# Single slots of an expert kernel: the next slot's rows are split ahead of two other copies, and one slot's row turns come later

## The chip, the core and the metric

The kernel runs on one core of a Trainium2 chip. The core has five engines with a program each: TensorE (PE; its weight loads are PEld), VectorE (DVE), ScalarE (ACT), GpSimd (POOL) and SyncE (SP). They meet only by semaphores, and each takes its own instructions in the order in which they were written. The metric is the device time of one execution in microseconds (us); less is better.

## The reference

Attention with rotary embedding, and behind it a layer of 8 experts of which each token takes one. Cut to what is computed:

```python
batch, n_heads, seq, head_dim = (8, 8, 576, 64)          # 4608 tokens of 512
scores = scale * np.matmul(q_rot, k_rot.transpose(0, 1, 3, 2))
attn = np.exp(scores - np.max(scores, axis=-1, keepdims=True)); attn /= attn.sum(-1, keepdims=True) + 1e-09
x = (attn @ v).transpose(0, 2, 1, 3).reshape(4608, 512)
e_idx = np.argmax(x @ w_gate, axis=1)                     # one expert of 8 for each token
for e in range(8):
    mask = e_idx == e
    h = np.maximum(x[mask] @ w1[e], 0.0)                  # 512 -> 1024
    out[mask] = gate_w[mask, None] * eom[mask, e, None] * (h @ w2[e])   # 1024 -> 512
```

## The kernel before

The first half of the execution is attention; the experts follow, and only they are touched by the change. The tokens of one expert are dealt into **slots**. A double slot takes 256 tokens (two halves h of 128), a **single** slot 128. Slots 0 to 4 are double and gather whole rows of tokens; slots 5 to 22 gather each token in quarters. Of these, 7, 9, 12, 15, 18 and 21 are single, the others double; every single slot is followed by a double one. (Three more slots stand behind a branch that depends on the data.)

All products are made of three float32r products: an operand is split into a high part (a cast on ACT) and a low part (the difference, on DVE), and high times high, low times high and high times low are added up in PSUM. A slot has eight **units** j, each with 512 KB of weights `wr`:

- Units 0 to 3 are the first layer (`first`, `products`): products of the slot's rows `xt` with the weights into `ph`, 24 matmuls a unit in a double slot (L1232, the rows stand as the moving operand in 256 columns), 12 in a single one (L1224). `ph` has two buffers in turn, for even and odd j. In a double slot ACT makes the high part `ht` with the ReLU (L1248) and DVE the low part (L1249); both read `ph`. In a single slot ACT copies the ReLU to `hr` (L1246), and a unit later `across` turns it on TensorE (L1259) and makes the high part on ACT (L1260) and the low part on DVE (L1261).
- Units 4 to 7 are the second layer (`second`, L1274): `ht` with the weights into `py`, 12 matmuls a unit in a double slot, 6 in a single one. After unit 7 `store` scales `py` into `y`, and GpSimd scatters it to the output.

Beside these each unit j of slot s does, in the order of `slot`: `split` of the weights six units ahead (the cast `wh` on ACT, L1159, and the difference `wl` on DVE, L1161), the load of the weights eight units ahead on SP's queue, `turns`, and `gathers`.

`turns` prepares the rows of the slots ahead. A half of gathered rows `xg` is transposed on DVE into `xr` (L1172, by `turned_in`); after the last half `gated` copies the gate factors `gs` (L1184). Then `turn` splits the half: `xt` high on ACT (L1193), `xt` low on DVE (L1194). Splitting is always done for the next slot, half h in unit 4+h, since there is only one `xt`, and the products of the current slot read it until the end of unit 3. The transposes are done two slots ahead in units 6 and 7 if the gather of that slot has been issued whole, and else one slot ahead in units 2 and 3. `gathers` issues up to two quarter gathers (L1118, on GpSimd, 128 tokens each) a unit, eight for a double slot; those of slot i wait until `gs` of slot i-2 is made, since both use one buffer.

Nothing orders the work but this text: the instructions of an engine stand in the order in which `slot` writes them.

Of the kernel before, what the change touches and what calls it, by code (L numbers as in the profile page):

```python
# [77 lines left out]
def list_rows(nb):  # L78
    return -(-nb * S // SLOT) * SLOT


def slot_counts(nb):


    n0 = min(5, -(-((nb - 2) * S - E * (SLOT - 1)) // SLOT)) if nb > 2 else 0
    n0 = max(0, n0)
    T = nb * S - n0 * SLOT
    n2 = max(0, -(-(T - E * P) // SLOT))
    most = (T + E * (P - 1)) // P
    if n2:  # L90
        n2 += 3
    return n0, n2, max(min(E, most - 2 * p) + 2 * max(0, p - n2) for p in range(most // 2 + 1))
# [40 lines left out]
class Small:  # L133


    def __init__(self, p):
        self.p, self.tag = p, "sc"
# [140 lines left out]
class Attention:  # L278
# [117 lines left out]
    def turns(self, g):  # L396
        n, i = divmod(g, 9)
        n -= i == 0
        if 0 <= n < len(self.pairs):
            for units in TURNS.get(i, ()):  # L400
                self.pairs[n].turn(units)


class Pair:
# [49 lines left out]
    def load(self, t):  # L454

        if t:
            self.raw = self.pp2.tile([P, 4, S], F32, tag="raw", name=f"raw{self.nm}")
        self.nc.sync.dma_start(out=self.raw[:, 2 * t:2 * t + 2, :], in_=self.qkd[:, 2 * t:2 * t + 2, :])
# [361 lines left out]
class Moe:  # L820
# [3 lines left out]
    def __init__(self, tc, nb, pools, cc, ident, cnt, w, xd, lists, lst, out):  # L824
        self.tc, self.nc, self.nb, self.NT = tc, tc.nc, nb, nb * S
        self.p1, self.px2, self.small = pools
        self.cc, self.ident, self.cnt, self.w, self.xd, self.lists, self.lst, self.out = cc, ident, cnt, w, xd, lists, lst, out
        self.n0, self.n2, self.n1 = slot_counts(nb)
        self.rows = list_rows(nb) // P
        self.idx, self.ei, self.quarters, self.xr = {}, {}, {}, {}  # L830
        self.due, self.sent, self.asked, self.gss_made = [], [], 0, set()
        self.wr, self.wp, self.xt, self.ht, self.gss, self.pys, self.hrs, self.regs = ({} for _ in range(8))

        self.T = max(1, self.n1 - 3)
        self.todo = [(2, 0, i) for i in range(self.n0)]

        k = 0
        for i in range(self.n2):
            self.todo.append((2, 2, i))
            while k < self.T and k * (self.n2 - 1) < i * self.T:  # L840
                self.todo.append((1, 1, k))
                k += 1
        self.todo += [(1, 1, i) for i in range(k, self.n1)]
        self.nm, self.end = "", self.n0 + self.n2 + self.T
# [255 lines left out]
    def gather(self, s, after=None):  # L1100
        if s >= self.end:
            return
        if not self.whole(s):
            for b in range(4 * self.todo[s][0]):
                self.part(s, b)
            return
        self.mark(self.xgs[s % 2][0:1, 0, 0:1], after)
        n = self.NT - 2 * S
        for h in range(self.todo[s][0]):
            self.nc.gpsimd.indirect_dma_start(  # L1110
                out=self.rows2[s % 2][:, h, :], out_offset=None, in_=self.xd[0:n, :],
                in_offset=bass.IndirectOffsetOnAxis(ap=self.ids(s, h), axis=0), bounds_check=n - 1, oob_is_err=False)
# [10 lines left out]
    def gathers(self, s, j):  # L1123

        if j == 6 and s + 2 < self.end and self.whole(s + 2):
            self.gather(s + 2)
        if j == 0:
            for i in range(max(self.asked + 1, s + 2), min(s + 4, self.end)):
                if not self.whole(i):
                    self.due += [(i, b) for b in range(4 * self.todo[i][0])]  # L1130
                    self.asked = i
        for _ in range(2):
            if self.due:
                i, b = self.due[0]
                if self.todo[i][1] in self.quarters and i - 2 in self.gss_made:
                    self.part(i, b)
                    self.due.pop(0)

    def load(self, u, after=None):
        if u >= 8 * self.end:  # L1140
# [52 lines left out]
        nc.scalar.copy(xth[:, :, hs], xr)  # L1193
        V.tensor_tensor(out=xtl[:, :, hs], in0=xr, in1=xth.bitcast(F32)[:, :, hs], op=ALU.subtract)  # L1194

    def turns(self, s, j):

        for i in (s + 1, s + 2):
            if i >= self.end:
                break  # L1200
            k, near = self.todo[i][0], i == s + 1
            for h in range(k):
                if self.whole(i):
                    now = near and j == h + 4
                else:
                    now = j == h + (2 if near else 6) and i not in self.gss_made
                    now = now and not any(g == i for g, _ in self.due) and (h == 0 or (i, 0) in self.xr)
                if now:
                    self.turned_in(i, h)
                    if h == (0 if self.whole(i) else k - 1):  # L1210
                        self.gated(i)
                if near and j == h + 4:
                    self.turn(i, h)
# [120 lines left out]
    def slot(self, s, left, per=2, last=False):  # L1334
        for j in range(8):
            u = 8 * s + j
            single = self.todo[s][0] == 1
            if j < 4:
                if s or j > 1 or not self.n0:
                    self.first(s, j)  # L1340
            elif not last:
                self.second(s, j - 4)
            if single and 1 <= j <= 4:
                self.across(s, j - 1)
            self.split(u + self.LEAD)
            self.load(u + self.LOADS)
            self.turns(s, j)
            if j == 7:
                self.close(s) if last else self.store(s)
            self.gathers(s, j)  # L1350
            if j == 0 and last:
                self.nc.gpsimd.drain()
            for _ in range(per if s or j > 1 else 1):
                if left:
                    left.pop(0)()
# [67 lines left out]
```

## Time and profile before

| | |
|---|---|
| median of 3 runs | 963.38 us (957.52 to 967.2) |
| the profiled execution | 959.85 us |
| its span, first to last instruction | 958.0 us |
| TensorE matmuls busy | 901.4 us (94%) |
| VectorE busy | 790.5 us (83%) |
| ScalarE busy | 657.4 us (69%) |
| GpSimd busy | 634.9 us (66%) |
| mean granted TensorE clock | 0.995 |

Busy times are averages over both halves of the program; which engine another one waits for at one place is seen in the timeline and in the list of waits. Times in rows count from the start of the span. In timelines a bracket shows how long the engine was idle before the instruction, and what ended that. A row may hold several instructions (x2), and a start-to-start distance is what one instruction costs the engine, since neighbours overlap a little at their ends.

### The profile page before, as it was taken

The page shows a single profiled execution, that of the slowest core. Times are in us where ns is not written, and L with a number is a line of the kernel's source. Part 1 is how long each engine was busy: PE and PEld are TensorE (multiplying, and loading weights), DVE is VectorE, ACT ScalarE, POOL GpSimd, SP SyncE. Part 2 cuts the span into 40 slices and gives each one's busy share as a digit, 9 for nine tenths or more (in the row PEclk, how much of TensorE's full clock was granted, in tenths as well). Part 3 has the DMA queues.
Part 4 walks back from the last instruction along what each step waited for, and adds up shares of the span by engine and source line. Part 5 has one row for each costly group of instructions (what it writes and reads, how often), then busy time and mean ns, then how long its engine had stood idle before and what let it go on. Part 6 is the DMA issues. An engine that isn't in the chain of part 4 may idle for free.

```text
span 958.0 us, 34278 instructions
## 1 busy us (share of the span) xinstructions
PE 901.4 (94%) x14325; PEld 779.5 (81%) x14325; DVE 790.5 (83%) x1456; ACT 657.4 (69%) x1373; POOL 634.9 (66%) x573
## 2 busy tenths in 40 slices
PE   4999998999999999989899999899999999999997
PEld 3777777778877777778788999799889998998986
DVE  6899998999999998989588777668886868778681
ACT  4777788899898988787764544447654657457561
POOL 4898898898989898798211228667847646476120
PEclk9999999999999999999999999999999999999999
DMA  6544565465646646455399957669796878878550
GB/s 239 196 177 143 189 225 200 166 237 188 229 148 228 234 153 212 141 203 176 114 344 309 304 188 233 222 213 308 264 295 230 288 234 274 284 237 275 199 184 21
DMA packets 61183, 208.44 MB, mean 218 GB/s; under 512 B 9512, under 2 KB 11614, under 8 KB 61024
## 3 DMA queue, kind: packets, MB, share of 16 engines
q1 hardware_dynamic: 49920, 183.78, 55.9%
q0 software_dynamic: 9824, 21.27, 6.4%
q8 instruction: 114, 1.87, 0.8%
q10 hardware_dynamic: 1280, 1.15, 0.4%
q14 instruction: 45, 0.37, 0.1%
HBM read 186.09 MB, written 22.43 MB: 218 GB/s over the span
## 4 chain that ended last, share of the span: by engine, by line
PE 63%; DVE 16%; issue 8%; ACT 7%; POOL 3%; DMA 2%; POOLq 0%; DVEq 0%; ACTq 0%
PE ph L1232 17%; PE py L1274 16%; PE acc L569 13%; PE sc L523 10%; DVE pm L532 7%; PE ph L1224 3%; ACT pm L539 3%; DVE pt L547 3%; PE acc L584 2%; DVE pt L545 2%; DVE xb L596 1%; DVE wl L1161 1%; POOL xg L1118 1%; DMA xg<-xd,2qi 1%; ACT ac L576 1%
## 5 line engine op out<-in xcount | busy, mean ns | idle before, releaser
L539 ACT ACTIVATE pm<-pm,m 128x576 f32<-128x576 f32 x288 | 221.7, 770 | 54.8 <-DVE pm L532 51.2
L1161 DVE TENSOR_TENSOR wl<-wr,wh 128x1024 fp32r<-128x1024 f32 x172 | 221.8, 1299 | 31.7 <-ACT wh L1159 29.8
L532 DVE TENSOR_SCALAR_CACHE_REDUCE pm<-sc 128x576 f32<-128x576 f32 x288 | 205.4, 746 | 24.6 <-PE sc L523 19.1
L569 PE MATMUL acc<-pt,v 32*64 32x128 f32 (+1 forms) x9216 | 197.3, 295 | 19.5 <-DVE xb L596 7.7
L1232 PE MATMUL ph<-xt,wh 128*128 128x256 f32 x1088 | 200.7, 286 | 8.1 <-DVE xt L1194 4.3
L1274 PE MATMUL py<-wh,ht 128*128 128x512 f32 x640 | 207.7, 396 | 0.0
L569 PEld LDWEIGHTS acc<-pt,v 32*64 32x64 f32 x9216 | 156.9, 131 | 45.1 <-issue 27.5
L1159 ACT CAST wh<-wr 128x1024 fp32r<-128x1024 f32 x184 | 187.6, 1047 | 0.0
L1232 PEld LDWEIGHTS ph<-xt,wh 128*128 128x128 f32 x1088 | 171.7, 192 | 11.6 <-DVE xt L1194 6.2
L523 PE MATMUL sc<-kq 64*128 64x288 f32 x1536 | 161.1, 320 | 16.4 <-ACT kq L484 9.8
L474 POOL TENSOR_TENSOR raw<-raw,rt 128x1152 f32<-128x1152 f32 x62 | 164.5, 2653 | 0.0
L523 PEld LDWEIGHTS sc<-kq 64*128 64x128 f32 x1536 | 122.0, 190 | 50.5 <-issue 22.2
L1232 PE MATMUL ph<-xt,wl 128*128 128x256 f32 x544 | 155.4, 286 | 0.0
L1118 POOL DMA_INDIRECT xg<-xd,2qi x96 | 120.8, 1259 | 49.7 <-issue 24.1
L1274 PEld LDWEIGHTS py<-wh,ht 128*128 128x128 f32 x640 | 120.4, 188 | 26.1
L1274 PE MATMUL py<-wl,ht 128*128 128x512 f32 x320 | 125.8, 393 | 0.0
L1248 ACT ACTIVATE ht<-ph 128x512 fp32r<-128x512 f32 x68 | 40.6, 597 | 117.8 <-PE ph L1232 117.8
L545 DVE STREAM_TRANSPOSE pt<-pm 128x576 f32<-128x576 f32 x160 | 116.9, 760 | 2.1 <-ACT pm L539 2.1
L1232 PEld LDWEIGHTS ph<-xt,wl 128*128 128x128 f32 x544 | 104.5, 192 | 0.1
L1249 DVE SCALAR_TENSOR_TENSOR ht<-ph,ht 128x512 fp32r<-128x512 f32 x68 | 47.0, 691 | 63.7 <-ACT ht L1248 63.5
L487 POOL TENSOR_TENSOR kq<-raw,kq 128x1152 fp32r<-128x1152 f32 (+1 forms) x33 | 82.5, 2500 | 9.1 <-ACT kq L484 9.0
L547 DVE STREAM_TRANSPOSE pt<-pm 128x1152 f32<-128x1152 f32 x64 | 88.0, 1374 | 0.7 <-ACT pm L539 0.7
(255 smaller groups left out, 1121.3 us busy)
## 6 DMA issues: line engine op xcount, KB each, us to landing
wr<-in_w SPq DMA_DIRECT2D x184, 512.0 KB, 4.6
raw<-in_qk SPq DMA_DIRECT2D x64, 576.0 KB, 4.9
v<-in_v SPq DMA_DIRECT2D x64, 576.0 KB, 6.3
xd<-xb SPq DMA_DIRECT2D x16, 640.0 KB, 4.0
xg<-xd,2qi POOLq DMA_INDIRECT x96, 4.6
xd<-xb SPq DMA_DIRECT2D x8, 160.0 KB, 4.8
rt<-in_rope ACTq DMA_DIRECT2D x1, 576.0 KB, 5.8
xg<-xd,1qi POOLq DMA_INDIRECT x24, 5.0
```

What stands on the lines that cost most here:

```text
L474: self.eng(eng).tensor_tensor(out=rv, in0=rv, in1=rt, op=ALU.mult)
L523: self.nc.tensor.matmul(self.ps[i][:, a, :HS], st, self.kq[r, mov, x], start=(n == 0), stop=(n == 2))
L532: self.nc.vector.tensor_scalar(self.halves(i), self.ps[i][:, :, :HS], 1.0, FAR, op0=ALU.mult, op1=ALU.min, accum_out=self.m[i])
L539: self.nc.scalar.activation(self.pc[i], self.pc[i], AF.Exp, bias=self.m[i], scale=-1.0, accum_out=self.z[:, zi:zi + 1])
L545: self.nc.vector.transpose(out=self.pt[:, c + 5 * h, :], in_=self.pc[units[0]])
L547: self.nc.vector.transpose(out=self.pt[:, c:c + 6:5, :], in_=self.pc[units])
L569: nc.tensor.matmul(self.acc[h * D:h * D + D, a, o:o + 32 * n], self.v[r, h, j, :], self.pt[r, u:u + n, 32 * j:32 * j + 32], start=(j == 0) ...
L1118: self.nc.gpsimd.indirect_dma_start(out=self.xgs[s % 2][:, b, :], out_offset=None, in_=self.xd.rearrange("n (q x) -> (n q) x", x=BW)[0:n, ...
L1159: self.nc.scalar.copy(wh, r)
L1161: eng.tensor_tensor(out=wl, in0=r, in1=wh.bitcast(F32), op=ALU.subtract)
L1232: nc.tensor.matmul(ph[:, f, :], st[:, dc, fs], mv[:, dc, :], start=(n == 0), stop=(n == 11))
L1274: self.nc.tensor.matmul(py[h], st[:, f, hs], mv, start=(f == 0 and n == 0), stop=(f == 7 and n == 2))
```

## The change

Two edits in the slots, with no instruction added or removed.

In single slots `turns` is called twice. For the next slot it is now called ahead of `across` and `split`, so that in units 4 and 5 the split of the next slot's rows stands ahead of the copies of the turned ReLU and of the weight casts of that unit. For the slot after the next the call stays where it was. Double slots keep their order.

`gathers` now notes in `asked_at` the unit in which a slot's last quarter was issued, and the transposes two slots ahead are only made if that was at least three units ago; the old test was that nothing of the slot was still due.

```diff
@@ gather
         if not self.whole(s):
             for b in range(4 * self.todo[s][0]):
                 self.part(s, b)
+            self.asked_at[s] = 8 * s - 8
             return
@@ gathers
                     self.part(i, b)
                     self.due.pop(0)
+                    if not any(g == i for g, _ in self.due):
+                        self.asked_at[i] = 8 * s + j
@@ turns
-    def turns(self, s, j):
+    def turns(self, s, j, ahead):
-        for i in (s + 1, s + 2):
-            if i >= self.end:
-                break
+        for i in (s + a for a in ahead if s + a < self.end):
             k, near = self.todo[i][0], i == s + 1
...
                     now = j == h + (2 if near else 6) and i not in self.gss_made
-                    now = now and not any(g == i for g, _ in self.due) and (h == 0 or (i, 0) in self.xr)
+                    now = now and i in self.asked_at and (near or 8 * s + j - self.asked_at[i] > 2) and (h == 0 or (i, 0) in self.xr)
@@ slot
+            if single:
+                self.turns(s, j, range(1, 2))
             if single and 1 <= j <= 4:
                 self.across(s, j - 1)
             self.split(u + self.LEAD)
             self.load(u + self.LOADS)
-            self.turns(s, j)
+            self.turns(s, j, range(2, 3) if single else range(1, 3))
```

Between the two programs the order differs on VectorE and ScalarE alone. The first place is the end of each single slot; here slot 9 on VectorE, units 3 to 5, before (`ht_9` is the low part of the slot's ReLU, `htp_3` the turned ReLU of unit 3, `xt_10` the rows of the next slot, `xr_0` and `xr_1` their halves):

```order
889 L1161 TENSOR_TENSOR wl_12410<-wr_12355,wh_12409 128x1024
890 L1261 TENSOR_TENSOR ht_9_12294<-htp_3_12422,ht_9_12293 128x2x128
891 L1161 TENSOR_TENSOR wl_12428<-wr_12387,wh_12427 128x1024
892 L1194 TENSOR_TENSOR xt_10_12434<-xr_0_12257,xt_10_12433 128x4x128
893 L1161 TENSOR_TENSOR wl_12444<-wr_12413,wh_12443 128x1024
894 L1194 TENSOR_TENSOR xt_10_12434<-xr_1_12277,xt_10_12433 128x4x128
```

The same place on VectorE with the change:

```order
889 L1164 TENSOR_TENSOR wl_12410<-wr_12355,wh_12409 128x1024
890 L1197 TENSOR_TENSOR xt_10_12423<-xr_0_12257,xt_10_12422 128x4x128
891 L1262 TENSOR_TENSOR ht_9_12294<-htp_3_12426,ht_9_12293 128x2x128
892 L1164 TENSOR_TENSOR wl_12432<-wr_12387,wh_12431 128x1024
893 L1197 TENSOR_TENSOR xt_10_12423<-xr_1_12277,xt_10_12422 128x4x128
894 L1164 TENSOR_TENSOR wl_12446<-wr_12413,wh_12445 128x1024
```

The first half of `xt_10` has passed one `ht_9` and one `wl`, the second half one `wl` more; the second half now has one weight difference less ahead of it. ScalarE at the same place, before:

```order
848 L1159 CAST wh_12409<-wr_12355 128x1024
849 L1260 CAST ht_9_12293<-htp_3_12422 128x2x128
850 L1159 CAST wh_12427<-wr_12387 128x1024
851 L1193 CAST xt_10_12433<-xr_0_12257 128x4x128
852 L1159 CAST wh_12443<-wr_12413 128x1024
853 L1193 CAST xt_10_12433<-xr_1_12277 128x4x128
```

ScalarE with the change:

```order
848 L1162 CAST wh_12409<-wr_12355 128x1024
849 L1196 CAST xt_10_12422<-xr_0_12257 128x4x128
850 L1261 CAST ht_9_12293<-htp_3_12426 128x2x128
851 L1162 CAST wh_12431<-wr_12387 128x1024
852 L1196 CAST xt_10_12422<-xr_1_12277 128x4x128
853 L1162 CAST wh_12445<-wr_12413 128x1024
```

The casts moved in the same way, ahead of the copy of the turned ReLU and of one weight cast each. The second place is slot 6, whose transposes are the only ones that move by the new test: before, they stand on VectorE in units 6 and 7 of slot 4. From unit 7 of slot 4 on, VectorE before (`y_11289` is the output of slot 4's second half):

```order
816 L1161 TENSOR_TENSOR wl_11277<-wr_11223,wh_11276 128x1024
817 L1172 STREAM_TRANSPOSE xr_1_11282<-xg 128x4x4x32
818 L1184 COPY gs_11284<-xg 32x2 x4
819 L1293 TENSOR_SCALAR y_11289<-py_1_11173,gs_10845 128x512
820 L1249 SCALAR_TENSOR_TENSOR ht_5_11305<-ph_0_11306,ht_5_11304 128x512
821 L1161 TENSOR_TENSOR wl_11334<-wr_11243,wh_11333 128x1024
```

VectorE with the change, from unit 7 of slot 4 to unit 3 of slot 5:

```order
815 L1164 TENSOR_TENSOR wl_11275<-wr_11223,wh_11274 128x1024
816 L1294 TENSOR_SCALAR y_11280<-py_1_11173,gs_10845 128x512
817 L1250 SCALAR_TENSOR_TENSOR ht_5_11296<-ph_0_11297,ht_5_11295 128x512
818 L1164 TENSOR_TENSOR wl_11325<-wr_11243,wh_11324 128x1024
819 L1250 SCALAR_TENSOR_TENSOR ht_5_11296<-ph_1_11345,ht_5_11295 128x512
820 L1164 TENSOR_TENSOR wl_11373<-wr_11278,wh_11372 128x1024
821 L1250 SCALAR_TENSOR_TENSOR ht_5_11296<-ph_2_11378,ht_5_11295 128x512
822 L1164 TENSOR_TENSOR wl_11406<-wr_11337,wh_11405 128x1024
823 L1175 STREAM_TRANSPOSE xr_0_11411<-xg 128x4x4x32
824 L1250 SCALAR_TENSOR_TENSOR ht_5_11296<-ph_3_11413,ht_5_11295 128x512
825 L1164 TENSOR_TENSOR wl_11441<-wr_11376,wh_11440 128x1024
826 L1175 STREAM_TRANSPOSE xr_1_11446<-xg 128x4x4x32
```

The two transposes of slot 6 and the copies of `gs` behind them have moved back by four units, behind three or four of the low parts `ht_5` that stood behind them.

## Rows read from the trace of the kernel before

**Rows 1.** Waits of TensorE from 480 us to the end: us, times, longest.

```profile
PE ph L1232 <- DVE xt L1194: 4.3, 6, 0.7
```

**Rows 2.** TensorE's timeline, slot 9 into 10: start, us, engine, line, operation.

```profile
695.07 0.40 PE L1274 MATMUL py<-wh,ht 128*128 128x512 f32 x1
695.30 0.28 PE L1232 MATMUL ph<-xt,wh 128*128 128x256 f32 x1
696.30 0.38 PE L1232 MATMUL ph<-xt,wh 128*128 128x256 f32 x1 [0.71 <-DVE xt L1194]
```

**Rows 3.** TensorE's timeline: first-layer ends of slots 8 and 22, behind singles 7 and 21.

```profile
659.53 0.28 PE L1232 MATMUL ph<-xt,wh 128*128 128x256 f32 x1
...
671.96 0.39 PE L1274 MATMUL py<-wh,ht 128*128 128x512 f32 x1
...
928.37 0.28 PE L1232 MATMUL ph<-xt,wh 128*128 128x256 f32 x1
...
940.74 0.40 PE L1274 MATMUL py<-wh,ht 128*128 128x512 f32 x1
```

**Rows 4.** TensorE's timeline: the first layer of slot 11, behind a double slot.

```profile
718.95 0.40 PE L1232 MATMUL ph<-xt,wh 128*128 128x256 f32 x2
...
730.39 0.40 PE L1274 MATMUL py<-wh,ht 128*128 128x512 f32 x1
```

**Rows 5.** VectorE's timeline at the end of slot 9.

```profile
691.16 1.23 DVE L1161 TENSOR_TENSOR wl<-wr,wh 128x1024 fp32r<-128x1024 f32 x1
692.30 0.42 DVE L1261 TENSOR_TENSOR ht<-htp,ht 128x256 fp32r<-128x256 f32 x1
692.67 1.23 DVE L1161 TENSOR_TENSOR wl<-wr,wh 128x1024 fp32r<-128x1024 f32 x1
693.82 0.68 DVE L1194 TENSOR_TENSOR xt<-xr,xt 128x512 fp32r<-128x512 f32 x1
694.42 1.22 DVE L1161 TENSOR_TENSOR wl<-wr,wh 128x1024 fp32r<-128x1024 f32 x1
695.55 0.69 DVE L1194 TENSOR_TENSOR xt<-xr,xt 128x512 fp32r<-128x512 f32 x1
...
700.37 0.69 DVE L1249 SCALAR_TENSOR_TENSOR ht<-ph,ht 128x512 fp32r<-128x512 f32 x1
```

**Rows 6.** ScalarE's timeline at the end of slot 9.

```profile
690.07 1.06 ACT L1159 CAST wh<-wr 128x1024 fp32r<-128x1024 f32 x1
...
692.54 0.62 ACT L1193 CAST xt<-xr 128x512 fp32r<-128x512 f32 x1
```

**Rows 7.** TensorE's timeline: the first layer of slot 5.

```profile
596.76 0.40 PE L1232 MATMUL ph<-xt,wh 128*128 128x256 f32 x2
...
606.44 0.39 PE L1232 MATMUL ph<-xt,wh 128*128 128x256 f32 x1 [3.76 <-DVE ht L1249]
...
613.80 0.40 PE L1274 MATMUL py<-wh,ht 128*128 128x512 f32 x1
```

**Rows 8.** VectorE's timeline at the end of slot 4.

```profile
603.74 0.71 DVE L1172 STREAM_TRANSPOSE xr<-xg 128x512 f32<-128x512 f32 x1 [3.98 <-DMA xg<-xd,2qi]
...
605.71 0.68 DVE L1249 SCALAR_TENSOR_TENSOR ht<-ph,ht 128x512 fp32r<-128x512 f32 x1
```

**Rows 9.** GpSimd's timeline: three of the gathers of slot 6.

```profile
590.91 1.00 POOL L1118 DMA_INDIRECT xg<-xd,2qi  x1 [0.31 <-issue]
...
593.52 3.55 POOL L1118 DMA_INDIRECT xg<-xd,2qi  x1 [0.30 <-issue]
...
598.68 1.95 POOL L1118 DMA_INDIRECT xg<-xd,2qi  x1 [0.30 <-issue]
```

**Rows 10.** Windows: stretch, length, busy of each engine, granted clock, DMA share, GB/s.

```profile
480.00:500.00 20.00, 20.00 (x125) 17.80 (x125) 15.75 (x28) 13.38 (x19) 2.91 (x3) 1.00 0.98 376
606.40:608.60 2.20, 2.16 (x11) 2.16 (x12) 2.20 (x3) 0.00 (x0) 1.73 (x2) 0.59 0.41 132
624.90:636.50 11.60, 11.60 (x98) 11.60 (x97) 6.50 (x7) 4.73 (x7) 7.62 (x7) 1.00 0.64 202
```

More of the change, by code (lines that the diff above doesn't have):

```diff
@@ L830, in __init__ @@
         self.idx, self.ei, self.quarters, self.xr = {}, {}, {}, {}
-        self.due, self.sent, self.asked, self.gss_made = [], [], 0, set()
+        self.due, self.sent, self.asked, self.gss_made, self.asked_at = [], [], 0, set(), {}
         self.wr, self.wp, self.xt, self.ht, self.gss, self.pys, self.hrs, self.regs = ({} for _ in range(8))
```

## The prediction

> **What bounds the kernel now.** I read the waits of TensorE first, since it has the most work, then its timeline around each wait, then VectorE, ScalarE and GpSimd at the same times. In the experts TensorE hardly pauses, and where it does the reader sees two places. The first comes six times: the first layer of the double slot behind each single slot waits for the low part of its rows, 4.3 us in all and 0.7 each [rows 1]. At slot 10 the first matmul starts at 695.30, needs only the high part, and runs; the second needs the low part and starts at 696.30 [rows 2], where 0.12 us later would have done (three matmuls of a first layer take 0.36 us: 96 of them take 11.44 us in slot 11, behind a double slot [rows 4]). The second place comes once: in slot 5 TensorE waits 3.76 us for VectorE's `ht` [rows 7], and VectorE had itself waited 3.98 us for a gather of slot 6, with this `ht` queued behind the transpose [rows 8].
>
> What each costs is read from the length of a first layer, which also holds what the waits do to the clock. Undisturbed it is 730.39 - 718.95 = 11.44 us [rows 4]. Behind the first single slot it is 671.96 - 659.53 = 12.43, behind the sixth and last 940.74 - 928.37 = 12.37 [rows 3]: 0.96 us more on average, times six 5.8 us. In slot 5 it is 613.80 - 596.76 = 17.04 [rows 7], so 5.6 us more, of which 3.76 are the wait and some 1.8 slower matmuls behind it, at a granted clock of 0.59, near the lower level of 1.2 GHz, where 1.00 is 2.4 GHz [rows 10]. Nothing else on the way to the end is touched, and TensorE's lead is passed on to the end one for one: behind the last slot's first layer stand only its second layer, one copy and the scatter.
>
> **Splits ahead in single slots.** Nothing is added, and on VectorE the queue at the end of slot 9 has no gap, so the new times come from moving its starts about [rows 5]. Start to start, `wl` takes 1.14 us (691.16 to 692.30), `ht` 0.37, `xt` 0.60. Before, the second `xt` starts at 695.55 and ends at 696.24; TensorE goes on 0.06 later. With the change: `wl` 691.16, first `xt` 692.30, `ht` 692.90, `wl` 693.27, second `xt` 694.41, end 695.10. That is 1.14 us earlier, one `wl`. TensorE wants it at 695.30 + 0.12 = 695.42 and can have it at 695.16. So the wait goes whole, with 0.26 us to spare. ScalarE must follow: its cast for the first half can start when `wh` ends at 690.07 + 1.06 = 691.13, takes 0.62 [rows 6] and is done at 691.75, ahead of 692.30. The cast overwrites `xt`, which the products of unit 3 read; that unit was over before TensorE began the 24 matmuls of 0.23 us (695.07 to 695.30 [rows 2]) that end at 695.30, so at about 689.6, and nothing new is waited for.
>
> What is pushed back is the `ht` of unit 3, 0.60 us on VectorE, to end at 693.3. TensorE wants it for the last six matmuls of the slot, which begin at 695.30 - 6 x 0.23 = 693.92: covered by 0.6 us. The weight differences that are passed belong to units six ahead and cost nothing.
>
> What is late next is the `ht` of the following slot's unit 0, at 700.37, ending at 701.06 [rows 5]. VectorE has the same work up to there and no gap in it, so it stays at 701.06 although TensorE comes 0.96 us sooner. It frees one of two `ph` buffers; TensorE wants that for unit 2, two units of 2.86 us behind 695.30, so at 701.02, and gets it at 701.06 + 0.06 = 701.12. Something like 0.1 to 0.2 us is lost again, in the four slots with two halves of rows two slots ahead (9, 12, 15, 18); behind slot 7 only one half is ahead and behind 21 none. I take 4 x 0.15 = 0.6 us. **Gain of this part: 5.8 - 0.6 = 5.2 us;** its bounds are nothing, if the wait only changes its place, and 5.8.
>
> **Slot 6 turned later.** The two transposes and the `gs` copies, some 2 us (from 603.74 to 605.71 stand one transpose, the copies and slot 4's `y` [rows 8]), leave the end of slot 4 for units 2 and 3 of slot 5. VectorE no longer stands in front of a gather that is still under way. What waited for it, `y`, its scatter and `ht`, goes on at once. At the new place the gathers have landed: the last one was there at 603.74 [rows 8], and TensorE ends unit 2 of slot 5 at 596.76 + 3 x 2.86 = 605.3, after which VectorE has an `ht` and a `wl` to make before the first of the transposes. The 2 us there lie beside TensorE's work: in the undisturbed first layer of slot 6 VectorE is busy 6.50 of 11.60 us [rows 10]. GpSimd's gathers of slot 8 use the buffer that these transposes read and can start only behind them, when slot 5 goes into its second layer; behind them in its queue stand slot 5's scatters and the gathers of slot 9. None is wanted before the end of slot 6, a double slot of some 23 us (11.44 for its first layer [rows 4], about as much for its second) later. So the 5.6 us go whole, and with the wait goes the clock's fall.
>
> How much of this is in every execution is the open size. The last gathers of slot 6 came late because one took 3.55 us on GpSimd, where another shortly before took 1.00 [rows 9]. Had it taken 1.00 as well, the wait would have been 2.55 us shorter, with no fall of the clock: 5.6 - 2.55 - 1.8 = 1.2 us. These are the bounds, 1.2 and 5.6. I take 5.6: the long gather starts at 593.52 and ends at 597.07 while VectorE works without a pause on its splits, and the next long one, 598.68 to 600.63 [rows 9], again lies beside a `wl`. That points to a cause in the order of the program and not in chance.
>
> The Trainium skill has the rule for that, in "SBUF — State Buffer", section "SBUF: two separate sides": VectorE and GpSimd share a pair of ports, held for a whole instruction, also by a VectorE operation with two SBUF inputs against a GpSimd one that reads SBUF. By that rule the long gather comes back in each execution and the gain is 5.6 us; without it, 1.2. The trace agrees only in part, since the 1.00 us gather lies beside splits as well.
>
> **The sum.** 5.2 + 5.6 = 10.8 us off the profiled execution, 959.85 - 10.8 = 949.1. That execution lies 3.5 us under the median of the runs, so from the median I expect 963.38 - 10.8 = 952.6 us.
>
> **The rivals.**
> *The gather is seldom so late.* Then only 1.2 us of the second part are there to be won: 5.2 + 1.2 = 6.4, 957.0 us. For it: one row of 3.55 among others of 1 to 2. Against it: the order that surrounds it is the same in every execution.
> *VectorE becomes the bound behind single slots.* The margins of 0.26 us and -0.1 are thin. If transposes and splits run 0.4 us later than moved starts say, half of the six waits comes back, at `xt` or at the following `ht`: 2.9 less, 955.5 us. For it: the queue without a gap from 691.16 to 700.37. Against it: the same instructions, whose total cannot grow by their order.
> *The splits gain nothing* because another wait ends just as late: 963.38 - 5.6 = 957.8 us. Against it: no other wait of TensorE is to be seen at these six places.
> *Slower.* The lower clock comes in at a place where TensorE now works without a pause. At it a first-layer matmul takes up to twice its 0.12 us, so each us of work costs another; from 10.8 us of work at the lower level on, the kernel is slower than before, and with twice that it takes 974 us. Against it: TensorE was busy 20 of 20 us from 480 to 500 at a clock of 1.00 [rows 10], and the waits that go are no rest that it needed there.
>
> **How the numbers follow.** The forecast has 0.56, the seldom late gather 0.17, VectorE as the bound 0.16, no gain from the splits 0.08, slower 0.03. The runs of before spread over 9.7 us, so a median of a few may be off by 2 to 3 us. The range goes from 949.5 (both parts at their upper bounds, 11.4, less a spread of 2.5) to 959 (the rival at 957.0 and 2 us of spread). One per cent, 9.6 us, is about what a measurement of this kernel can tell from no change. The forecast's gain lies only 1.2 us beyond it, so about one in five of its own chance falls short by the spread, and the rivals with smaller gains reach it now and then: faster by over 1% 0.54, within 1% 0.43, slower 0.03.
>
> **What would show it.** In the new profile the six waits of the first layer for `xt` are gone, the first layers behind single slots last about 11.5 us, slot 5's too, the clock is 1.00 around 605 us, and the end of VectorE's second `xt` lies 0.1 to 0.3 us ahead of the first matmul that needs it. A new wait of some 0.1 us for `ht` in unit 2 may stand in four slots. The prediction is wrong if waits for `xt` or `ht` of 0.5 us remain, if VectorE still waits for a gather in slot 5, or if TensorE's clock falls elsewhere.

## The result, and the profile after

The changed kernel takes 951.61 us, the median of 6 runs (946.07 to 953.68), against 960.86 us for 6 runs of the kernel before (957.52 to 967.2). The ratio is 0.9892, with a 95% interval of 0.9859 to 0.9926, so about 1% faster; the two medians differ by 9.25 us, 0.96%. Times here and below are medians of all runs of a kernel, while a ratio and its interval are those of its fast runs and not the quotient of two medians. The forecast was 952.6 us. The profiled execution of the changed kernel took 952.37 us, its span 950.6 us.

The list of waits of TensorE from 480 us to the end holds no first layer any more; one wait of 0.3 us is left, at 522.60, and the kernel before has it as well. The six waits for `xt` [rows 1] and the wait for `ht` of slot 5 [rows 7] are gone:

```profile
PE pl L718 <- DVE xt L1197: 0.3, 1, 0.3
```

TensorE's timeline of the changed kernel shows the first layer of slot 5 (answers to [rows 7]), of slot 10 with its third unit (to [rows 2]) and of slot 22 (to [rows 3]); the last row of each is the start of its second layer:

```profile
599.90 0.40 PE L1233 MATMUL ph<-xt,wh 128*128 128x256 f32 x2
...
611.42 0.40 PE L1275 MATMUL py<-wh,ht 128*128 128x512 f32 x1
...
692.07 0.40 PE L1233 MATMUL ph<-xt,wh 128*128 128x256 f32 x2
...
697.67 0.28 PE L1233 MATMUL ph<-xt,wl 128*128 128x256 f32 x1
697.84 0.51 PE L1233 MATMUL ph<-xt,wh 128*128 128x256 f32 x2
...
703.69 0.39 PE L1275 MATMUL py<-wh,ht 128*128 128x512 f32 x1
...
921.85 0.40 PE L1233 MATMUL ph<-xt,wh 128*128 128x256 f32 x2
...
933.36 0.39 PE L1275 MATMUL py<-wh,ht 128*128 128x512 f32 x1
```

Slot 5 takes 611.42 - 599.90 = 11.52 us where it took 17.04, slot 10 takes 11.62, slot 22 11.51. At 692.07 the first two matmuls run as one group; in [rows 2] the second came 1.00 us behind the first.

VectorE's timeline of the changed kernel at the end of slot 4 (answers to [rows 8]) and of slot 9 (to [rows 5]):

```profile
602.67 0.75 DVE L1294 TENSOR_SCALAR y<-py,gs 128x512 f32<-128x512 f32 x1
603.67 0.69 DVE L1250 SCALAR_TENSOR_TENSOR ht<-ph,ht 128x512 fp32r<-128x512 f32 x1 [0.25 <-ACT ht L1249]
...
611.45 0.70 DVE L1175 STREAM_TRANSPOSE xr<-xg 128x512 f32<-128x512 f32 x1
...
687.93 1.23 DVE L1164 TENSOR_TENSOR wl<-wr,wh 128x1024 fp32r<-128x1024 f32 x1
689.07 0.68 DVE L1197 TENSOR_TENSOR xt<-xr,xt 128x512 fp32r<-128x512 f32 x1
689.67 0.42 DVE L1262 TENSOR_TENSOR ht<-htp,ht 128x256 fp32r<-128x256 f32 x1
690.01 1.22 DVE L1164 TENSOR_TENSOR wl<-wr,wh 128x1024 fp32r<-128x1024 f32 x1
691.14 0.68 DVE L1197 TENSOR_TENSOR xt<-xr,xt 128x512 fp32r<-128x512 f32 x1
...
697.09 0.69 DVE L1250 SCALAR_TENSOR_TENSOR ht<-ph,ht 128x512 fp32r<-128x512 f32 x1
```

In slot 5 the first transpose of slot 6's rows stands at 611.45, behind TensorE's whole first layer, and `y` and the `ht` of the first three units no longer queue behind it. In slot 9 the second `xt` ends at 691.14 + 0.68 = 691.82, ahead of the first product.

ScalarE's casts of `xt` there (answers to [rows 6]) are early enough: the second ends at 690.15, and VectorE needs it at 691.14.

```profile
689.51 0.64 ACT L1196 CAST xt<-xr 128x512 fp32r<-128x512 f32 x1
```

GpSimd's gathers of slot 6 (answers to [rows 9]) still hold a long one, right behind a short one:

```profile
596.46 0.99 POOL L1119 DMA_INDIRECT xg<-xd,2qi  x1 [0.30 <-issue]
597.76 2.79 POOL L1119 DMA_INDIRECT xg<-xd,2qi  x1 [0.30 <-issue]
```

The long one ends at 600.55, 0.95 us behind the start of VectorE's first operation with one input behind the splits, here a small cast with other small operations behind it:

```profile
599.60 0.15 DVE L906 CAST 1idx<-1tr 128x9 int32<-128x9 f32 x1
```

The windows of the changed kernel (answers to [rows 10]; columns as there) have the granted clock at 1.00, the 2.4 GHz level, in the first layer of slot 5 and over the whole of the experts:

```profile
599.90:611.40 11.50, 11.50 (x97) 11.50 (x96) 8.95 (x17) 4.84 (x7) 8.79 (x8) 1.00 0.90 277
...
476.20:933.40 457.20, 456.80 (x2946) 414.66 (x2945) 356.63 (x552) 264.30 (x368) 236.24 (x181) 1.00 0.78 256
```

The two profiled executions differ by 7.5 us, the experts alone by more. From the first product of the experts to the end of the last first layer it was 473.30 to 940.74 before, 467.44 us, and is 476.24 to 933.36 now, 457.12 us: 10.3 us less. The half ahead of the experts, which the change does not touch, took 2.9 us longer in this execution; in the other profiles below its end lies anywhere from 472.07 to 477.91, whatever the order. So the experts' stretch is the better measure of the change in a single profile, and the table of the experiments gives it for each kernel.

### The profile page after: what moved, and what is told of

Same layout as the page of the kernel before. It is cut to its first block, busy times and chain, and to the rows that moved or that the text cites. A ratio compares the mean times of both kernels' runs of the same rounds, so it can differ in the third digit from the quotient of the medians.

```text
span 950.6 us, 34288 instructions
## 1 busy us (share of the span) xinstructions
PE 903.2 (95%) x14325; PEld 782.2 (82%) x14325; DVE 791.8 (83%) x1456; ACT 657.2 (69%) x1373; POOL 635.0 (67%) x573
## 3 DMA queue, kind: packets, MB, share of 16 engines
q8 instruction: 114, 1.87, 0.8%
## 4 chain that ended last, share of the span: by engine, by line
PE 67%; DVE 13%; issue 9%; ACT 5%; POOL 2%; DMA 2%; POOLq 0%; DVEq 0%; ACTq 0%
PE py L1275 18%; PE ph L1233 17%; PE acc L569 14%; PE sc L523 11%; DVE pm L532 6%; PE ph L1225 3%; PE acc L584 2%; ACT pm L539 2%; DVE pt L547 2%; DVE pt L545 2%; DVE xb L596 1%; DMA xg<-xd,2qi 1%; ACT ac L576 1%; PE acc L718 1%; DMA rt<-in_rope 1%
## 5 line engine op out<-in xcount | busy, mean ns | idle before, releaser
L1164 DVE TENSOR_TENSOR wl<-wr,wh 128x1024 fp32r<-128x1024 f32 x172 | 219.5, 1288 | 29.8 <-ACT wh L1162 27.5
L1233 PE MATMUL ph<-xt,wh 128*128 128x256 f32 x1088 | 198.2, 285 | 0.0
L523 PE MATMUL sc<-kq 64*128 64x288 f32 x1536 | 163.1, 323 | 15.9 <-ACT kq L484 9.5
```

Source lines behind the costliest of these rows:

```text
L523: self.nc.tensor.matmul(self.ps[i][:, a, :HS], st, self.kq[r, mov, x], start=(n == 0), stop=(n == 2))
L1164: eng.tensor_tensor(out=wl, in0=r, in1=wh.bitcast(F32), op=ALU.subtract)
L1233: nc.tensor.matmul(ph[:, f, :], st[:, dc, fs], mv[:, dc, :], start=(n == 0), stop=(n == 11))
```

## The experiments

First-layer lengths are start to start, as above; "behind singles" are the six of slots 8, 10, 13, 16, 19 and 22. Ratios are to the kernel before on the same chip. A time marked (one) is that of a single run.

| kernel | time, us | ratio, 95% | slot 5 | behind singles | experts |
|---|---|---|---|---|---|
| before, first profile | 960.86 | 1 | 17.04 | 12.37 to 12.49 | 467.44 |
| before, again | 959.00 (one) | | 15.28 | 12.35 to 12.47 | 465.83 |
| changed, first profile | 951.61 | 0.9892 [0.9859, 0.9926] | 11.52 | 11.51 to 11.63 | 457.12 |
| changed, again | 951.44 | 0.9921 [0.9884, 0.9957] | 11.52 | 11.51 to 11.63 | 456.77 |
| later turning alone | 955.23 | 0.9946 [0.9923, 0.9968] | 11.52 | 12.36 to 12.46 | 461.86 |
| order alone | 955.20 | 0.9950 [0.9930, 0.9971] | 14.00 | 11.52 to 11.62 | 459.64 |
| low part made twice | 954.79 | 0.9952 [0.9917, 0.9988] | 11.51 | 11.94 to 12.35 | 460.70 |
| parts behind the relu copy | 951.95 | 0.9902 [0.9869, 0.9935] | 11.52 | 11.52 to 11.64 | 456.97 |
| fills in slot 4 | 963.52 (one) | | 15.45 | 12.36 to 12.47 | 466.44 |
| transposes in slot 4 | 957.01 (one) | | 13.21 | 12.35 to 12.46 | 464.25 |

**The two halves, a first time.** Four kernels ran together first, on a chip on which the kernel before took 973.21 us (965.8 to 986.43). The first one has the new rule for turning alone:

```diff
-            if single:
-                self.turns(s, j, range(1, 2))
...
-            self.turns(s, j, range(2, 3) if single else range(1, 3))
+            self.turns(s, j, range(1, 3))
```

> Only the new test on the gather; the order in single slots is the old one. My theory: the first layer of slot 5 lasts 11.5 us instead of 17.0, the clock stays at 1.00 there, and the six first layers behind single slots still last 12.4 us with their waits of 0.7 us for xt. About 5.5 us off the time of before (ratio near 0.994). Rival, that the late gather is seldom so late and the profile of before was an unlucky one: the median falls by 1 to 2 us only.

The second has the new order alone, with the old condition:

```diff
-                    now = now and i in self.asked_at and (near or 8 * s + j - self.asked_at[i] > 2) and (h == 0 or (i, 0) in self.xr)
+                    now = now and not any(g == i for g, _ in self.due) and (h == 0 or (i, 0) in self.xr)
```

> Only the order in single slots; the old test on the gather. My theory: the six waits are gone and the six first layers last 11.5 to 11.6 us, in all 5.1 us off (ratio near 0.995); slot 5 keeps its wait, VectorE waits 2 to 4 us for a gather of slot 6, and the first layer of slot 5 lasts 14 to 17 us, with a slower clock behind the wait if that is over 3 us. The rival, chance, expects that the wait in slot 5 is under 1.5 us in this execution, with no gather of slot 6 over 2.1 us on GpSimd.

Measured: 976.66 us, ratio 1.0021 [0.9971, 1.0072], and 970.87 us, ratio 0.998 [0.9939, 1.0021]. The places themselves did mostly as expected: with the rule alone slot 5 took 11.52 and five of the six behind singles 12.35 to 12.47 (one 13.15); with the order alone four of the six took 11.51 to 11.63, the others 12.11 and 12.51. One expectation failed: with the order alone slot 5 took 11.52 us and not 14 to 17, and no gather of slot 6 took over 1.87 us, which is what the rival expected. Slot 4 ahead of it had taken 16.53 us, though, so that in this execution the gathers were done by 595.94, and VectorE's splits began only at 600.82: it does not tell the two apart. Both kernels show waits of TensorE in double slots for which the profile names no releaser, which neither earlier profile has, 7.7 us of them in the first layers of the first kernel and 4.2 us in those of the second. The timed ratios of this pair say nothing on the change as long as these stand in them.

**Only unit 5 early.** The changed kernel, with the early turning in unit 5 of a single slot alone, so that the first half's parts stand where they stood before:

```diff
-            if single:
+            early = single and j == 5
+            if early:
                 self.turns(s, j, range(1, 2))
...
-            self.turns(s, j, range(2, 3) if single else range(1, 3))
+            self.turns(s, j, range(2, 3) if early else range(1, 3))
```

> The changed kernel, but in single slots the split of the next slot's rows is called early in unit 5 only, not in unit 4. My theory: the low part of the second half ends when all that stands ahead of it is done, so only the one weight difference that it passes in unit 5 counts; the first half's place in unit 4 changes nothing. First layers behind single slots last 11.5 to 11.6 us as in the changed kernel, same time as that. The rival, that both moves share the gain, expects 11.9 to 12.0 us at the six places and some 2.5 us more in all.

Measured: 962.31 us, ratio 0.9916 [0.9865, 0.9966]; behind singles 11.51 to 11.68 in four slots, 11.96 and 12.45 in two beside waits without a releaser. Where nothing else disturbs, the one `wl` that the second half passes is enough.

**Nothing turned two slots ahead in a single slot.** The changed kernel with another condition:

```diff
-                    now = now and i in self.asked_at and (near or 8 * s + j - self.asked_at[i] > 2) and (h == 0 or (i, 0) in self.xr)
+                    now = now and i in self.asked_at and (near or self.todo[s][0] == 2 and 8 * s + j - self.asked_at[i] > 2) and (h == 0 or (i, 0) in self.xr)
```

> The changed kernel, but single slots make no transposes two slots ahead; they come in units 2 and 3 of the following double slot. My theory: the 0.1 us by which the first layers of slots 10, 13, 16 and 19 still exceed 11.5 us comes from the low part of ht in unit 0 queued behind two transposes and the copies of gs; with these away, these four last 11.45 to 11.52 us, 0.4 us less in all, too little for the times. The rival, that the rest has another cause (the split itself), expects 11.6 us as before. If the later gathers that hang on gs come too late, a wait for a gather appears in the double slots and the kernel is slower by that.

Measured: 982.49 us, ratio 1.0119 [1.0053, 1.0185]. In two of the four slots, 13 and 19, the first layer took 11.52 and 11.48, as expected; in the two others 12.05 and 11.99. But this kernel has the most of the waits without a releaser, 15.0 us in first layers, in seven places. Row of TensorE's timeline, then of ScalarE's, in slot 6 of this kernel:

```profile
644.82 0.80 PE L1233 MATMUL ph<-xt,wh 128*128 128x256 f32 x2 [3.29 <-issue]
```

```profile
643.44 0.60 ACT L1249 ACTIVATE ht<-ph 128x512 fp32r<-128x512 f32 x1 [5.75 <-remote]
```

TensorE waits for the `ph` that ScalarE's `ht` frees. ScalarE has been idle for 5.75 us when it starts that `ht`, although the last product into this `ph` had ended some 4.8 us before, at about 638.6. What ScalarE waits for is not in the records. Whether this edit adds to it stays open, since it ran only there.

**Both kernels once more**, on another chip:

> The kernel before, unchanged, in a second profile beside the others. Theory (the order of VectorE's and ScalarE's work sets both waits): the six first layers behind single slots again take 12.35 to 12.5 us where nothing else delays the slot ahead of them, with a wait of 0.7 us for the second xt each; slot 5's first layer is again 15 to 17 us if the gathers of slot 6 are asked for at the same place. Rival for slot 5 (the late gather was chance): slot 5 takes 11.5 us here. If first layers of double slots also show waits of TensorE that the profile of the first execution did not have (as in the order-only and rule-only kernels), these waits belong to the chip and not to an edit.

> The changed kernel, unchanged, in a second profile and timed beside the others. Theory: first layers behind single slots 11.5 to 11.6 us, slot 5 11.5 us, no wait for xt or for xg; about 10 us (1.0%) under the kernel before if that one keeps slot 5's stall on this chip, about 5 us (0.5%) if it does not.

Measured: 959.0 us for the one profiled run of before (19 more runs of it there have a median of 959.92), 951.44 for the changed kernel, ratio 0.9921. No wait without a releaser is in either profile. The stall of slot 5 is back in the kernel before, with another size; TensorE's timeline:

```profile
597.80 0.40 PE L1232 MATMUL ph<-xt,wh 128*128 128x256 f32 x2
...
605.74 0.50 PE L1232 MATMUL ph<-xt,wh 128*128 128x256 f32 x2 [2.08 <-DVE ht L1249]
...
613.08 0.40 PE L1274 MATMUL py<-wh,ht 128*128 128x512 f32 x1
```

The long gather is back too, 2.79 us this time. GpSimd's and VectorE's timelines of that execution:

```profile
595.67 2.79 POOL L1118 DMA_INDIRECT xg<-xd,2qi  x1 [0.30 <-issue]
```

```profile
596.37 1.21 DVE L1161 TENSOR_TENSOR wl<-wr,wh 128x1024 fp32r<-128x1024 f32 x1
597.51 0.69 DVE L1172 STREAM_TRANSPOSE xr<-xg 128x512 f32<-128x512 f32 x1
...
603.04 0.71 DVE L1172 STREAM_TRANSPOSE xr<-xg 128x512 f32<-128x512 f32 x1 [1.89 <-DMA xg<-xd,2qi]
```

It ends at 598.46, 0.95 us behind the transpose at 597.51, the first operation with one input behind the splits.

**The two halves, a second time**, the same edits on a third chip:

> The later turning of slot 6 alone (the rule on asked_at; the order in single slots as before), on another day beside the other half. Theory (two separate causes): slot 5's first layer 11.5 us, the six behind singles keep 12.35 to 12.5 us with 0.7 us of wait for xt; 4 to 6 us under the kernel before (ratio 0.994 to 0.996). Rival (the splits' order does the work): slot 5 stays at 15 us or more, ratio 1.000. If TensorE's waits of 0.4 us and more that name no releaser, which the first execution of this kernel had in double slots, are gone here, they belong to the chip it ran on.

> The order in single slots alone (high and low parts ahead of the relu copies and weight casts; the old rule for turning two slots ahead). Theory: the six first layers behind singles 11.5 to 11.65 us, slot 5 keeps its wait for xg (2 to 4 us, first layer 15 to 17 us); about 5 us under the kernel before (ratio 0.995). Rival (singles keep waiting, or the gain depends on the rule): 12.4 us each, ratio 1.000.

Measured: 955.23 us, ratio 0.9946 [0.9923, 0.9968], and 955.20 us, ratio 0.9950 [0.9930, 0.9971]; there are no waits without a releaser. Rule alone, TensorE's timeline: slot 5 has no wait and slot 10 waits as before.

```profile
600.48 0.40 PE L1233 MATMUL ph<-xt,wh 128*128 128x256 f32 x2
...
612.00 0.40 PE L1275 MATMUL py<-wh,ht 128*128 128x512 f32 x1
...
694.49 0.39 PE L1233 MATMUL ph<-xt,wh 128*128 128x256 f32 x1 [0.71 <-DVE xt L1197]
```

Order alone, TensorE's timeline: slot 5 waits, and slot 10 takes 11.62 us.

```profile
603.93 0.51 PE L1233 MATMUL ph<-xt,wh 128*128 128x256 f32 x2 [2.28 <-DVE ht L1250]
...
690.38 0.40 PE L1233 MATMUL ph<-xt,wh 128*128 128x256 f32 x2
...
702.00 0.39 PE L1275 MATMUL py<-wh,ht 128*128 128x512 f32 x1
```

Each half does its own part and none of the other's. With the order alone slot 5's 14.00 us are less than the 15 to 17 expected, while VectorE's wait for the gather, 2.15 us, lies in its range. The two gains add up to 1.04%; the whole was measured at 1.08% and 0.79%, and the kernel with the parts behind the relu copy, whose lengths are the same, at 0.98%.

**The low part made twice.** The changed kernel, with 0.60 us more of VectorE's work ahead of the second `xt` in single slots:

```diff
+        for _ in range(2 if h == 0 and self.todo[s - 1][0] == 1 else 1):
-        V.tensor_tensor(out=xtl[:, :, hs], in0=xr, in1=xth.bitcast(F32)[:, :, hs], op=ALU.subtract)
+            V.tensor_tensor(out=xtl[:, :, hs], in0=xr, in1=xth.bitcast(F32)[:, :, hs], op=ALU.subtract)
```

> The changed kernel with the low part of the first half made twice in single slots: 0.60 us more of VectorE's work ahead of the second xt. Theory (the second xt comes 0.26 us ahead of its need in the changed kernel): the spare is used up, so TensorE waits 0.3 to 0.4 us for xt behind each of six single slots, first layers there 11.85 to 12.0 us, with the pushed-back ht some 3 to 4 us in all (0.35%). Rival (VectorE has time to spare behind single slots, and it was ScalarE's half of the reordering that counted): first layers stay at 11.5 to 11.6 us and the time does not change.

Measured: 954.79 us; the experts take 460.70 us against 456.77 for the changed kernel beside it, 3.9 more. TensorE's timeline at slot 10:

```profile
689.44 0.28 PE L1234 MATMUL ph<-xt,wh 128*128 128x256 f32 x1
689.98 0.39 PE L1234 MATMUL ph<-xt,wh 128*128 128x256 f32 x1 [0.26 <-DVE xt L1198]
```

VectorE's timeline ahead of it, the two low parts of the first half:

```profile
686.45 1.41 DVE L1198 TENSOR_TENSOR xt<-xr,xt 128x512 fp32r<-128x512 f32 x2
```

The wait is back with 0.26 to 0.29 us in all six places. From start to start the second matmul comes 0.54 us behind the first instead of 0.12, so 0.42 late. The added operation costs 1.41 - 0.68 = 0.73 us and not 0.60, so some 0.31 us were spare. The first layers grow by 0.46 and 0.43 us behind slots 7 and 21, which is this delay, and by 0.72 to 0.75 in the other four, where `ht` is pushed back as well; there they are longer than the 12.0 us expected, and the 3.8 us in all are as expected.

**Parts behind the relu copy.** The changed kernel, with the early turning moved behind the relu copy but still ahead of the casts:

```diff
-            if single:
-                self.turns(s, j, range(1, 2))
             if single and 1 <= j <= 4:
                 self.across(s, j - 1)
+            if single:
+                self.turns(s, j, range(1, 2))
```

> The changed kernel, with the high and low parts moved behind the relu copy of unit 3 but still ahead of the weight casts. Theory (it is the one weight cast that the second xt is moved ahead of that counts): the second xt ends at the same distance ahead of TensorE's need, first layers behind singles 11.45 to 11.65 us, the same time as the changed kernel. Rival (being ahead of the relu copies is part of the gain): a wait for xt of about 0.3 us returns behind each of the six single slots, first layers of 11.9 to 12.3 us, 3 to 4 us in all.

Measured: 951.95 us, ratio 0.9902 [0.9869, 0.9935], the same lengths as the changed kernel. VectorE's timeline at the end of slot 9:

```profile
689.11 0.42 DVE L1262 TENSOR_TENSOR ht<-htp,ht 128x256 fp32r<-128x256 f32 x1
689.44 0.68 DVE L1197 TENSOR_TENSOR xt<-xr,xt 128x512 fp32r<-128x512 f32 x1
690.04 1.22 DVE L1164 TENSOR_TENSOR wl<-wr,wh 128x1024 fp32r<-128x1024 f32 x1
691.17 0.68 DVE L1197 TENSOR_TENSOR xt<-xr,xt 128x512 fp32r<-128x512 f32 x1
```

The second `xt` stands as in the changed kernel; only the first one and `ht` have changed places. Going ahead of the relu copy gains nothing, going ahead of the split of the weights gains all. Whether VectorE's order would do it without ScalarE's was not tried.

**Why the gather is long: fills.** The kernel before, with a small fill behind each operation with two inputs in slot 4:

```diff
+        if 38 <= u < 46:
+            self.gap()
...
+        if s == 5:
+            self.gap()
...
+        self.nc.vector.memset(self.regs['gap'], 0.0)
```

> Only slot 4 differs from the kernel before: behind each of its two-input operations on VectorE a fill of a 128x128 scratch tile follows. Theory (a run of two-input operations on VectorE holds GpSimd's gathers back): no gather of slot 6 takes over 2.1 us (one took 3.55 us before), VectorE's wait for xg falls from 4.0 us to under 2.5 us and slot 5's first layer from 17.0 to 15 us or less. Rival (the gather is long by its own DMA or by chance, whatever VectorE does): a gather of about 3 us stays among the eight of slot 6 and slot 5 takes 16 to 17 us.

Measured: slot 5 takes 15.45 us, between what the theory and the rival expected, and the long gather stays. GpSimd's and VectorE's timelines:

```profile
599.12 3.67 POOL L1118 DMA_INDIRECT xg<-xd,2qi  x1 [0.30 <-issue]
```

```profile
599.99 0.17 DVE L1169 MEMSET gap<- 128x128 f32 x1
600.09 0.61 DVE L1201 TENSOR_TENSOR xt<-xr,xt 128x512 fp32r<-128x512 f32 x1
600.68 0.17 DVE L1169 MEMSET gap<- 128x128 f32 x1
600.77 1.15 DVE L1161 TENSOR_TENSOR wl<-wr,wh 128x1024 fp32r<-128x1024 f32 x1
601.89 0.17 DVE L1169 MEMSET gap<- 128x128 f32 x1
601.99 0.64 DVE L1179 STREAM_TRANSPOSE xr<-xg 128x512 f32<-128x512 f32 x1
```

The theory's expectation failed: two fills passed while the gather stood, and it ended at 602.79, behind the third fill and the transpose. Either the theory is wrong or a fill that holds VectorE for 0.1 us opens nothing. The next kernel tells.

**Why the gather is long: transposes.** The kernel before; the transpose of slot 5's rows, with one input, is made again on both sides of each low part:

```diff
+        if s == 5:
+            V.transpose(out=xr.rearrange("p d (b j) -> p b d j", j=Q), in_=x)
         V.tensor_tensor(out=xtl[:, :, hs], in0=xr, in1=xth.bitcast(F32)[:, :, hs], op=ALU.subtract)
+        if s == 5:
+            V.transpose(out=xr.rearrange("p d (b j) -> p b d j", j=Q), in_=x)
```

> The kernel before; in slot 4 the transposition of slot 5's rows (one input, 0.7 us on VectorE) is made again ahead of and behind each of the two low parts of xt, in the same place in memory, so that no run of two-input operations there is longer than 1.2 us (3.1 to 4.8 us before). Theory (a run of two-input operations on VectorE holds a gather back until the first one-input operation behind it): no gather of slot 6 over 2.3 us, and each that is over 1.3 us ends 0.9 to 1.0 us behind the start of a one-input operation. Rival (gathers are long for another reason): one of 2.8 to 3.7 us stays, as in all other executions of this order.

Measured: no gather of slot 6 over 1.92 us. GpSimd's and VectorE's timelines:

```profile
594.69 1.92 POOL L1118 DMA_INDIRECT xg<-xd,2qi  x1 [0.30 <-issue]
```

```profile
594.53 1.21 DVE L1161 TENSOR_TENSOR wl<-wr,wh 128x1024 fp32r<-128x1024 f32 x1
595.66 0.69 DVE L1196 STREAM_TRANSPOSE xr<-xg 128x512 f32<-128x512 f32 x1
...
602.41 0.69 DVE L1172 STREAM_TRANSPOSE xr<-xg 128x512 f32<-128x512 f32 x1
```

The gather starts beside a `wl` and ends at 596.61, 0.95 us behind the transpose that follows. The row at 602.41 has no wait for a gather any more. Slot 5 still takes 13.21 us, but here VectorE itself is late with 4 x 0.7 us of added work, so the length is no measure of what a short gather alone would save.

## Why the prediction was right

**Splits ahead in single slots, 5.2 us.** The first layers behind singles lost 5.07 us between the two profiles (74.53 to 69.46 in sum), and the order alone measured 0.50% of 960.58, 4.8 us (2.8 to 6.7). The mechanism is the one worked out: the second `xt` comes one `wl` earlier, and that is all that it passes. It ends at 691.82 where TensorE wanted it at 692.07 + 0.12 = 692.19, and with the 0.06 us from its end to TensorE's start some 0.31 us are spare; doing the low part twice gave the same, where the prediction had 0.26. The `ht` of unit 3 that is pushed back cost nothing, and leaving it in its place gained nothing. The part of the change that goes ahead of the relu copies is without effect; the prediction did not split it off, and had no number on it.

**The 0.6 us that is lost again.** It is there, and smaller: `ht` of unit 0 ends at 697.09 + 0.69 = 697.78, TensorE's third unit starts at 697.84, 0.17 behind the matmul before it instead of 0.12. The four slots take 11.58 to 11.63 us, the two others 11.51 and 11.53: some 0.3 us in all.

**Slot 6 turned later, 5.6 us.** Slot 5 went from 17.04 to 11.52 us, 5.5 us; the rule alone measured 0.54% of 960.58, 5.2 us (3.1 to 7.4). In the other executions of the old turning the excess over 11.44 was 15.28 - 11.44 = 3.8 us and, with the order alone, 14.00 - 11.44 = 2.6 us. All three excesses, 5.6 us in the first profile, 3.8 and 2.6, lie between the prediction's bounds of 1.2 and 5.6, and the value that it took is the largest of them: that 5.6 us was right for the two first profiles is in part luck. Two things vary: the wait (3.76, 2.08 and 2.28 us) and the clock behind it. Windows of the kernel before, again, right behind its wait, and of the order alone:

```profile
605.70:607.90 2.20, 2.16 (x15) 2.16 (x16) 2.20 (x3) 0.00 (x0) 1.73 (x2) 0.84 0.47 130
607.90:610.00 2.10, 2.10 (x12) 2.10 (x11) 0.66 (x1) 0.00 (x0) 1.65 (x2) 0.50 0.76 279
```

```profile
603.90:606.10 2.20, 2.17 (x18) 2.17 (x19) 2.20 (x3) 0.00 (x0) 1.72 (x2) 1.00 0.44 132
```

After 2.08 us of wait the granted clock went down to 0.50, the 1.2 GHz level, after 2.28 us it stayed at 1.00: beside the wait itself, the stall cost 1.8 us more in the one execution and 0.3 in the other. The 3 us that an expectation above names for the clock are therefore no line that these runs show: it fell behind the shorter of the two waits.

**"A cause in the order of the program and not in chance."** This holds for the gather. In ten profiles, the eight of the table whose slot 4 is as before and the two with work added there, a gather of slot 6 was held back (1.92 to 3.67 us). In eight of the ten it ended 0.94 to 0.95 us behind the start of the first one-input operation after the splits; the exceptions are the fills, and the kernel with the low part made twice, where one gather came through between two splits.

The gathers of all slots show the same. In the kernel before, 74 of 128 started while VectorE was in a `wl` or an `xt`, whose two inputs both lie in SBUF, and took 1.00 to 3.55 us. Another 53 started beside nothing, beside an operation with one input, or beside an `ht`, one of whose inputs lies in PSUM, and none of them took over 1.14 us. That limit is the same in the other thirteen profiles.

The Trainium skill, "SBUF — State Buffer", section "SBUF: two separate sides", has a rule that fits: VectorE and GpSimd share a pair of ports, which one of them holds for a whole instruction, a VectorE operation with two SBUF inputs included where the GpSimd operation reads SBUF. The transposes agree with it (the gather ended 0.95 us behind one of them). But the gather was held back over up to three operations in a row and not over one, and the fills, 0.1 us each, do not show an opening; why is not shown.

But the step from "the long gather comes back" to "the whole 5.6 us come back" was too short: the changed kernel has the long gather too, with 2.79 us, and loses nothing. What costs is a VectorE that stands in its queue until the gather has landed, and how long it stands varies.

**The rivals.** VectorE did not become the bound behind singles; the doubled low part shows how near it is, at 0.3 us. The splits alone do gain, against the rival that gave them nothing. The seldom late gather has a little truth, as a size: the gather is not seldom late, but its stall is smaller in the other executions. The clock did not fall where TensorE now works through: 1.00 over the whole of the experts.

**The sum.** 10.8 us were forecast. The profiles give 10.3 us in the experts, the ratio 1.08% of 960.86, 10.4 us (7.1 to 13.5). Later measurements give 7.6 us (changed, again) and 9.4 us (parts behind the relu copy). The level was forecast from a median of 963.38, which with more runs is 960.86; a time below the forecast therefore does not mean that more was gained, and that it lies within 1.0 us of the forecast is in part luck. The prediction gave 0.54 to a gain of over 1% and 0.43 to one within it; the three measurements, 1.08, 0.79 and 0.98%, have intervals that hold 1%, so they do not settle which it is.

## What to carry to other kernels

When an engine's queue runs without a gap, look for the one instruction in it that another engine waits for, and count which of the instructions ahead of it are wanted later: here one weight difference of 1.14 us, passed in six places, was worth 5 us, and the other moves at the same places were worth nothing. A prefetch step that waits for its own transfer belongs where nothing urgent is queued behind it; then a long transfer costs nothing, as the 2.79 us gather of the changed kernel shows. And a stall read in one execution is one draw: 5.6, 3.8 and 2.6 us here, because the wait varies and what the clock adds behind it comes and goes.

## What was not expected of the hardware

A gather issued by GpSimd while VectorE works through a run of operations with two SBUF inputs (`wl`, `xt`, `wl`) was let in at a boundary between them in one of eight profiles; with fills of 0.1 us at the boundaries it was not let in at the first two. It ended 0.94 to 0.96 us behind the start of the next operation with one input, a transpose or a cast of 0.15 us with others behind it, whether 1.92 or 3.65 us after its own start. In the shorter run before it (`wl`, `xt`) a gather that started 0.02 us ahead of the `xt` (590.91 in [rows 9], the `xt` at 590.93) was not held and took 1.00 us.

On one chip TensorE's first layers waited 3.0 to 15.0 us, in each of four kernels, with no releaser named, and ScalarE stood idle for up to 7.2 us ahead of an `ht`. The kernel before was not profiled there; its fastest run of 29 took 965.8 us, against 952.01 to 957.52 us elsewhere. Both halves, run again on another chip, show none of it. Its cause stays open.
